# Eight heads at a time in an attention and feed-forward kernel, and identity products ahead of the first scores

## The chip, the cores and the metric

The kernel runs on one core of a Trainium2 chip. The metric is the device time of one execution in microseconds; the kernel before takes 1137.74 us (median of three runs, 1136.55 to 1138.45).

## The reference

A transformer block with adaptive LayerNorm. S = 2048 tokens, D = 1024, 32 query heads of width 32 that share one key and one value head, feed-forward width F = 3584, all in bf16. Cut to what matters:

```python
mod = (silu(c) @ w_mod).reshape(1, 6, 1, -1)      # sa, ca, ga, sb, cb, gb
h = layernorm(x) * (1 + ca) + sa
q = (h @ wq) -> 32 heads;  k = h @ wk;  v = h @ wv
p = softmax(q k^T / sqrt(32))
x = x + ga * ((p v) @ wo)
h = layernorm(x) * (1 + cb) + sb
return x + gb * ((silu(h @ w1) * (h @ w3)) @ w2)
```

## The kernel before

**Tiles.** The queries are cut into NB = 8 blocks of 256 tokens. `QT[:, n, f, :]` holds, for block n, four heads (f of 8) of 32 rows each, transposed: partition 32 g + d is row d of head g. `KT` holds the transposed keys four times over, once for each strip of 32 partitions. `V[:, k, :]` holds the values of key tile k (16 tiles of 128 keys). The normalised input, transposed, is `HT`; after the projections its memory is used again for feed-forward tiles.

**Attention.** The list `CYC` names 512 steps (n, f, j), each with four heads, 256 queries and 256 keys. For each step `s_exp` issues a burst of eight score products on TensorE: four heads in four row strips side by side, first for one key tile and then for the other, into four of the six PSUM banks of `S6`. Then come two exponentials on ScalarE (128x1024 each) into `U`, a ring of NU = 10 steps. Eight steps with one f are a unit (`av`): `pairs` adds the two key tiles of two steps on VectorE (128x2048), folds of 128x1024 bring these sums down, `dens` multiplies the last one by ones (row sums), `av_mm` multiplies `U` by `V` in four column strips, and `attend` transposes the row sums, takes their reciprocal, transposes back, copies the products from PSUM and writes their quotient over `QT[:, n, f]`. Units 0 and 1 run together in `two_units`.

**Rest of a block.** `wo` multiplies the eight `QT` tiles by the scaled output weights (32 products of 512 columns), adds to `X1`, and normalises; `slab` (14 a block) makes gate and up products, with a tanh on ScalarE for the silu; `quarter` (4 a block) multiplies by w2. The feed-forward of a block runs while the next block's attention does. Everything beside scores uses PSUM banks 6 and 7, until the last exponentials set the other six free.

**Order.** `Graph.op` collects operations with their dependences, an estimated time and a due time `vt`. `Placer` plays them through with these times and writes each engine's program in the order found, with semaphore waits. An operation may have several engines (`alts`); the one that starts first takes it. TensorE works in three array forms, "S" (scores, row strips), "A" or "C" (column strips) and "F" (whole array), and `SWITCH` prices a change between them. `PLAN` has 65 entries, one for each eight score steps: slacks for the choice and offsets on due times by tag and engine ("an/dve", "d10/sp"). Early projections carry estimates of their own (`cold`, 0.95, 1.7).

**The start.** Fourteen DMAs on the SyncE queue bring x, two fields of w_mod and wq in an order that the plan sets (tags d0 to d13). `lnt1` normalises a tile of 128 tokens and transposes it on TensorE; for tiles 0 to 5 the transposes go into the `S6` banks. `mod_cols` computes the scale and shift fields by products of one column, `scale0` scales the weights, `k_proj` and `q_proj` fill `KT` and `QT`. The first scores need tiles 0 and 1, both fields and the first two groups of wq.

Of the kernel before, what the change touches and what calls it, by code (L numbers as in the profile page):

```python
# [4 lines left out]
F32 = mybir.dt.float32  # L5
ACT = mybir.ActivationFunctionType
ALU = mybir.AluOpType
# [35 lines left out]
class Graph:  # L43
# [64 lines left out]
    def alias(self, new, old):  # L108
# [8 lines left out]
    (0, 0.08, 0.14, 0, 1.1, {"an/dve": 11, "av/dve": 9, "d0/sp": -38, "d1/sp": 10, "d10/sp": 222, "d11/sp": 2,  # L117
     "d12/sp": -4, "d13/sp": 2, "d2/sp": 51, "d3/sp": -151, "d6/sp": 67, "d7/sp": 32, "d8/sp": -29, "ev/act": -21,
     "k/pe": -26, "k/dve": 40, "ln/pe": -51, "ln/act": 32, "ln/dve": -11, "ln/pool": 57, "mc/pe": 57, "mc/sp": -2,
     "mod/pe": -62, "mod/dve": 10, "nm/act": 79, "pair/dve": -129, "q/pe": 3, "q/dve": -57, "quarter/pe": 11,  # L120
     "quarter/dve": -2, "s/pe": 67, "s/act": -3, "slab/pe": -5, "slab/act": 81, "slab/dve": 30, "v/pe": -8,
     "v/pool": 19, "wo/pe": -78, "wo/dve": 1, "wo/sp": 36}),
    (0, 0.11, 0.18, 2, 1.1, {"an/dve": 8, "av/pe": -111, "av/dve": 2, "d0/sp": -31, "d1/sp": 16, "d10/sp": -68,
     "d12/sp": 63, "d13/sp": -1, "d3/sp": -14, "d5/sp": 2, "d7/sp": -26, "d8/sp": -2, "ev/act": -29, "k/pe": -36,
     "k/dve": -9, "kb/pe": 72, "mod/dve": -5, "nm/act": 32, "pair/dve": -106, "q/pe": -4, "q/dve": -32,
     "quarter/dve": 2, "s/pe": 55, "s/act": 107, "slab/pe": -26, "slab/dve": 33, "slab/sp": 94, "v/pool": -34,
     "wo/pe": -77, "wo/dve": 4, "wo/pool": -59, "wo/sp": 22, "d11/sp": 0, "ln/pe": 0, "mod/pe": 0, "slab/act": 0}),
    (0, 0.25, 0.29, 0, 1.1, {"av/dve": 9, "d0/sp": -58, "d1/sp": 20, "d10/sp": 257, "d11/sp": -6, "d13/sp": 2,
     "d3/sp": -2, "d4/sp": 1, "d8/sp": 83, "ev/act": -11, "k/pe": -49, "k/dve": 1, "kb/dve": -7, "mc/pe": 63,
     "mc/sp": 5, "nm/act": 30, "out/sp": 1, "s/act": 114, "slab/sp": 4, "v/dve": 3, "v/pool": -26, "wo/pe": -78,  # L130
     "wo/dve": 14, "wo/pool": -23, "an/dve": 0, "d12/sp": 0, "d2/sp": 0, "mod/dve": 0, "pair/dve": 0,
     "quarter/pe": 0, "wo/sp": 0, "d5/sp": 0}),
    (0, 0.12, 0.29, 0, 3.5, {"an/dve": -3, "av/pe": -6, "av/dve": 6, "d12/sp": 20, "d4/sp": -21, "d9/sp": -6,
     "ev/act": -1, "k/pe": -62, "kb/dve": -3, "ln/pe": -2, "mc/pe": 77, "mod/dve": -9, "q/pe": -2, "q/dve": -56,
     "s/act": 2, "sc/dve": -14, "slab/act": 78, "slab/dve": 30, "slab/sp": 6, "wo/dve": 19, "d11/sp": 0,
     "mc/sp": 0, "s/pe": 0, "v/pool": 0, "wo/pe": 0, "wo/pool": 0, "out/sp": 0}),
    (0, 0.12, 0.21, 2, 2.5, {"an/dve": 49, "av/pe": -4, "d0/sp": -31, "d1/sp": 1, "d13/sp": -2, "d4/sp": -6,
     "d8/sp": 90, "ev/act": 38, "k/dve": -3, "mc/pe": 79, "nm/act": -1, "pair/dve": -93, "quarter/pe": 9,
     "slab/act": 70, "slab/dve": 33, "slab/sp": 18, "v/dve": -69, "v/pool": -4, "wo/pe": -6, "wo/dve": 1,
     "av/dve": 0, "d12/sp": 0, "k/pe": 0, "ln/dve": 0, "q/pe": 0, "d9/sp": 0, "sc/dve": 0}),  # L140
    (0, 0.12, 0.19, 1, 0.7, {"an/dve": -2, "av/pe": -8, "av/dve": 6, "d0/sp": -2, "d1/sp": 16, "d11/sp": 27,
     "d4/sp": -37, "d7/sp": -25, "k/pe": 1, "kb/pe": 5, "kb/dve": -4, "ln/pe": 4, "mc/pe": 143, "q/dve": -69,
     "quarter/pe": 12, "sc/dve": -12, "slab/pe": -27, "slab/dve": 32, "slab/sp": 13, "v/dve": 1, "wo/dve": 6,
     "wo/pool": 17, "d10/sp": 0, "mod/dve": 0, "nm/act": 0, "s/act": 0, "v/pool": 0}),
    (0, 0.12, 0.28, 0, 0.6, {"d10/sp": -68, "d3/sp": -46, "d8/sp": 83, "d9/sp": 72, "kb/pe": 2, "ln/dve": -11,
     "mc/pe": -7, "pair/dve": -16, "q/dve": -85, "q/sp": -6, "quarter/pe": 4, "slab/act": 82, "slab/dve": 33,
     "slab/sp": 16, "wo/pe": -5, "wo/dve": 3, "wo/pool": 15, "an/dve": 0, "d11/sp": 0, "v/pe": 0, "kb/dve": 0,
     "sc/dve": 0}),
    (0.16, 0.02, 0.28, 0, 2.1, {"av/dve": -2, "d10/sp": -85, "d11/sp": 1, "d4/sp": -32, "d5/sp": -18,
     "ev/act": -15, "kb/pe": -4, "ln/pe": -20, "ln/dve": -8, "ln/pool": 7, "mc/pe": 9, "mc/sp": 16, "mod/dve": -4,  # L150
     "nm/act": -31, "pair/dve": -79, "q/pe": -13, "quarter/pe": 2, "slab/pe": -22, "slab/dve": 31, "slab/sp": -62,
     "wo/pool": -40, "d0/sp": 0, "d7/sp": 0, "k/pe": 0, "slab/act": 0}),
    (0.14, 0.19, 0.09, 1, 2.1, {"d0/sp": -46, "d1/sp": 3, "d10/sp": -68, "d13/sp": 1, "d3/sp": -17, "d4/sp": -54,
     "d7/sp": -25, "d8/sp": 78, "k/pe": -1, "ln/dve": -11, "mc/pe": -28, "mc/dve": 25, "mod/pe": 4, "nm/act": -29,
     "pair/dve": -90, "q/pe": -2, "q/dve": -81, "quarter/pe": -10, "sc/dve": -1, "v/pe": -3, "v/dve": 5,
     "wo/pool": -18, "d11/sp": 0, "ev/act": 0, "mc/sp": 0, "mod/dve": 0, "d5/sp": 0, "kb/pe": 0}),
    (0.14, 0.17, 0.24, 1, 2.1, {"av/pe": -4, "d1/sp": 31, "d3/sp": 24, "d7/sp": -35, "ev/act": 20, "kb/pe": 6,
     "ln/dve": -16, "ln/pool": 60, "mc/pe": 2, "mc/dve": 35, "nm/act": -28, "pair/dve": -28, "q/dve": -49,
     "quarter/pe": -1, "slab/act": 10, "v/dve": 20, "wo/pool": -13, "av/dve": 0, "d0/sp": 0, "mod/pe": 0,
     "q/pe": 0, "slab/pe": 0}),  # L160
    (0.14, 0.16, 0.29, 1, 2.1, {"an/dve": -8, "d0/sp": -2, "d10/sp": -63, "d3/sp": 19, "d4/sp": -106, "kb/pe": 13,
     "ln/pe": 35, "ln/pool": 24, "mc/pe": -59, "mc/sp": -30, "mod/pe": 1, "nm/act": -45, "out/sp": -3,
     "pair/dve": 6, "q/pe": 4, "quarter/pe": 5, "sc/dve": 36, "v/pool": -11, "wo/sp": 1, "ln/act": 0, "mc/dve": 0}),
    (0.14, 0.16, 0.25, 1, 2.8, {"an/dve": -14, "d10/sp": -74, "d11/sp": -67, "d3/sp": -62, "d4/sp": -104,
     "d7/sp": -26, "ev/act": 41, "k/pe": 9, "kb/dve": 14, "ln/pe": 31, "ln/pool": -6, "nm/act": -24,
     "pair/dve": -10, "sc/dve": -24, "slab/pe": 4, "slab/dve": 21, "slab/sp": -61, "wo/pool": -17, "d0/sp": 0,
     "mc/sp": 0, "q/pe": 0, "slab/act": 0, "v/dve": 0}),
    (0.09, 0.26, 0.19, 1, 2.8, {"an/dve": -45, "d0/sp": -7, "d1/sp": 39, "d10/sp": -83, "d3/sp": 2, "d4/sp": -54,
     "d7/sp": -35, "k/pe": -94, "k/dve": -10, "kb/pe": 2, "ln/pe": -10, "ln/pool": -7, "mc/pe": -9, "mc/dve": 3,
     "nm/act": -23, "pair/dve": -3, "q/pe": -109, "quarter/pe": -3, "slab/dve": -32, "v/pool": -5, "wo/pe": -20,  # L170
     "d11/sp": 0, "slab/pe": 0, "av/pe": 0, "slab/sp": 0, "kb/dve": 0}),
    (0.09, 0.16, 0.25, 0, 2.8, {"d0/sp": -1, "d10/sp": -85, "d5/sp": -74, "k/dve": -7, "ln/pe": 4, "mc/pe": -11,
     "mc/sp": 2, "nm/act": -24, "pair/dve": -15, "slab/dve": -33, "v/dve": 1, "an/dve": 0, "d1/sp": 0, "ln/dve": 0,
     "quarter/pe": 0, "kb/pe": 0}),
    (0, 0.22, 0.2, 1, 2.4, {"d0/sp": 49, "d4/sp": -29, "k/pe": -87, "k/dve": -10, "mc/pe": -15, "nm/act": -13,
     "q/pe": -48, "slab/dve": -11, "slab/sp": -52, "v/dve": 2, "wo/pe": -83, "wo/dve": -12, "pair/dve": 0,
     "v/pool": 0, "d5/sp": 0}),
    (0, 0.13, 0.15, 1, 3.5, {"av/dve": -5, "d0/sp": 1, "d10/sp": -68, "d4/sp": -56, "d9/sp": 73, "k/pe": -82,
     "kb/pe": 4, "ln/pe": 16, "mc/pe": -12, "mc/sp": 14, "q/pe": -38, "slab/dve": 101, "slab/sp": 13, "wo/pe": -60,
     "d3/sp": 0, "ev/act": 0, "sc/dve": 0}),  # L180
    (0, 0.16, 0.15, 1, 3.1, {"av/dve": -7, "d10/sp": -70, "d11/sp": 19, "d4/sp": -25, "ev/act": 41, "k/pe": -32,
     "ln/pe": -17, "mc/pe": -16, "nm/act": -34, "pair/dve": -41, "slab/pe": -11, "slab/act": -11, "slab/sp": 4,
     "v/dve": -4, "wo/pe": -61, "slab/dve": 0, "kb/pe": 0, "wo/pool": 0}),
    (0.09, 0.14, 0.26, 1, 2.6, {"an/dve": -16, "av/dve": -5, "d11/sp": 14, "d12/sp": 26, "d3/sp": 64, "d4/sp": -22,
     "d5/sp": 13, "ev/act": 123, "k/pe": -87, "kb/pe": 25, "mod/dve": 2, "nm/act": -31, "pair/dve": -7,
# [400 lines left out]
def build(nc, x_in, wq_in, wk_in, wv_in, wo_in, w1_in, w3_in, w2_in, c_in, wmod_in, out, S, D, F):  # L586
# [110 lines left out]
    def pe_mm(n, cnt):  # L697
        return cnt * (n / 2400.0 + 0.0026) + 0.002
# [685 lines left out]
```

## Time and profile before

| | |
|---|---|
| median of three runs | 1137.74 us (1136.55 to 1138.45) |
| profiled execution | 1137.71 us, its span 1135.9 us |
| TensorE, VectorE, ScalarE busy | 1108.3, 992.1, 1021.3 us |
| TensorE clock granted | 0.998 of full, mean |
| DMA | 209.72 MB, mean 185 GB/s |
| first exponential starts | 33.74 us |
| last exponential ends | 1036.3 us |

In the views PE is TensorE, PEld its weight loads, DVE VectorE, ACT ScalarE, POOL GpSimd and SP SyncE. All operations are recorded by one helper, so every row shows L22, and groups are told apart by tiles: `S<-QT,KT` are scores, `U<-S` exponentials, `PB<-U,V` the P·V products, `PB<-PS,ONES` the row sums, `PS<-U` pairs and `PS<-PS` folds. The feed-forward products read `H20` in `HT` or `QT`, in which the normalised rows of the block before are kept. A row of the timeline has start, time, engine, operation, out<-in, array rows and columns, moving operand and count; a bracket tells how long the engine sat idle before it and who released it. Products overlap, so the time between two starts says more than the time of one.

### The profile page before, as it was taken

To read this page: it belongs to the slowest core of one execution; us is meant where nothing else is said; L and a number is where in the kernel's file an instruction comes from. 1 tells how busy PE (TensorE), PEld (TensorE's weight loads), DVE (VectorE), ACT (ScalarE), POOL (GpSimd) and SP (SyncE) were. 2 spreads that over 40 slices of the span, in tenths; PEclk is the share of its full clock that TensorE was granted. 3 is DMA by queue.
4 is the path that set the end of the run, shared out by engine and by line. 5 is a ranking of instruction groups with operands and counts; after the bars stand their busy time and mean duration, and the time that the engine had idled before them with its cause. 6 is when DMAs were issued, how large, how long until landed. Compare 5 with 4: busy or idle time off the path is not lost.

```text
span 1135.9 us, 38650 instructions
## 1 busy us (share of the span) xinstructions
PE 1108.3 (98%) x17512; PEld 757.2 (67%) x17512; DVE 992.1 (87%) x1614; ACT 1021.3 (90%) x1158; POOL 41.3 (4%) x92
## 2 busy tenths in 40 slices
PE   6899999999999999999999999999999999999998
PEld 6644446666567766777567766777577756776887
DVE  7988999998999889998998899988998889987532
ACT  5999999999999999999999999999999999994110
POOL 5200000000000000000000000000000000000000
PEclk9999999999999999999999999999999999999999
DMA  9320397665486658865596577768597568777993
GB/s 345 106 76 5 128 263 191 175 193 140 114 258 195 174 131 216 235 193 152 128 283 194 149 198 190 219 195 222 130 274 202 150 159 218 207 201 197 246 242 92
DMA packets 381540, 209.72 MB, mean 185 GB/s; under 512 B 17600, under 2 KB 373184, under 8 KB 381376
## 3 DMA queue, kind: packets, MB, share of 16 engines
q1 hardware_dynamic: 380944, 207.11, 65.8%
q8 instruction: 138, 2.26, 0.8%
q14 instruction: 26, 0.21, 0.1%
q10 hardware_dynamic: 432, 0.13, 0.0%
HBM read 199.89 MB, written 4.19 MB: 180 GB/s over the span
## 4 chain that ended last, share of the span: by engine, by line
PE 61%; ACT 25%; DVE 11%; issue 1%; POOL 1%; DMA 0%; DVEq 0%
PE PB L22 44%; ACT U L22 24%; PE S L22 16%; DVE PS L22 4%; DVE ST L22 2%; ACT HT L22 1%; DVE QT L22 1%; POOL RS L22 1%; DVE X L22 1%; DVE HT L22 1%; DVE RB L22 1%; DVE XNB L22 0%; DMA X<-in_A_x_dram 0%; DVE MV L22 0%; DVE RC L22 0%
## 5 line engine op out<-in xcount | busy, mean ns | idle before, releaser
L22 ACT ACTIVATE U<-S 128x1024 bf16<-128x1024 f32 x1024 | 964.6, 1131 | 7.2 <-PE S L22 6.3
L22 DVE TENSOR_TENSOR PS<-U 128x2048 bf16<-128x2048 bf16 x256 | 307.3, 1217 | 9.4 <-ACT U L22 7.9
L22 DVE TENSOR_TENSOR PS<-PS 128x1024 bf16<-128x1024 bf16 (+1 forms) x420 | 282.5, 690 | 3.4
L22 PE MATMUL PB<-QT,W 128*128 128x256 bf16 (+1 forms) x2992 | 229.8, 273 | 1.2 <-DVE HT L22 1.0
L22 PE MATMUL S<-QT,KT 32*128 32x256 bf16 x4096 | 203.8, 273 | 8.0 <-ACT U L22 5.0
L22 PEld LDWEIGHTS PB<-QT,W 128*128 128x128 bf16 (+1 forms) x2992 | 172.3, 97 | 44.3 <-issue 26.5
L22 PE MATMUL PB<-W2S,HT 128*128 128x256 bf16 x1512 | 188.4, 273 | 0.0
L22 PEld LDWEIGHTS PB<-W2S,HT 128*128 128x128 bf16 x1512 | 137.8, 98 | 39.4 <-issue 21.3
L22 PEld LDWEIGHTS S<-QT,KT 32*128 32x128 bf16 x4096 | 60.7, 92 | 139.8 <-ACT U L22 130.1
L22 PE MATMUL PB<-U,V 128*32 128x256 bf16 x4096 | 127.4, 273 | 0.9 <-ACT U L22 0.5
L22 PE MATMUL PB<-QT,HT 128*32 128x256 bf16 (+1 forms) x1560 | 116.0, 273 | 1.5 <-DVE HT L22 1.1
L22 PEld LDWEIGHTS PB<-U,V 128*32 128x32 bf16 x4096 | 101.6, 96 | 21.2 <-issue 12.7
L22 PE MATMUL PB<-HT,W 128*32 128x512 bf16 (+3 forms) x896 | 101.2, 336 | 0.1
L22 PEld LDWEIGHTS PB<-QT,HT 128*32 128x32 bf16 (+1 forms) x1560 | 85.3, 97 | 23.5 <-issue 14.1
L22 ACT ACTIVATE HT<-PB 128x512 bf16<-128x512 f32 (+1 forms) x105 | 74.4, 708 | 12.3 <-PE PB L22 12.3
L22 DVE SCALAR_TENSOR_TENSOR HT<-HT,PB 128x512 bf16<-128x512 bf16 x101 | 69.0, 684 | 8.1 <-ACT HT L22 8.0
L22 PEld LDWEIGHTS PB<-HT,W 128*32 128x32 bf16 (+1 forms) x896 | 51.1, 98 | 33.4 <-issue 10.5
L22 DVE TENSOR_TENSOR HT<-HT,PB 128x512 bf16<-128x512 bf16 x99 | 67.4, 681 | 2.5 <-PE PB L22 1.6
L22 ACT ACTIVATE HT<-S 128x512 bf16<-128x512 f32 (+1 forms) x16 | 11.5, 730 | 54.6 <-PE S L22 54.6
L22 DVE STREAM_TRANSPOSE RB<-PB 128x256 f32<-128x256 f32 x63 | 28.0, 444 | 37.3 <-PE PB L22 36.8
L22 PE MATMUL PB<-WO,QT 128*128 128x512 bf16 (+1 forms) x248 | 56.0, 381 | 1.1 <-DVE RB L22 1.1
L22 POOL TENSOR_SCALAR RS<-MV 128x1 f32<-128x1 f32 x32 | 11.6, 362 | 1004.5 <-DVE MV L22 1003.4
(107 smaller groups left out, 669.5 us busy)
## 6 DMA issues: line engine op xcount, KB each, us to landing
W<-in_B_w_dram SPq DMA_DIRECT2D x150, 512.0 KB, 4.6
W2S<-in_B_w_dram SPq DMA_DIRECT2D x30, 1792.0 KB, 8.5
HT<-in_B_w_dram SPq DMA_DIRECT2D x74, 512.0 KB, 4.6
W2S<-in_w_mod_dram SPq DMA_DIRECT2D x8, 1024.0 KB, 5.7
X<-in_A_x_dram SPq DMA_DIRECT2D x8, 512.0 KB, 7.5
U<-in_w_mod_dram SPq DMA_DIRECT2D x4, 1024.0 KB, 12.1
out_dram<-X SPq DMA_DIRECT2D x7, 512.0 KB, 7.4
W2S<-in_A_x_dram SPq DMA_DIRECT2D x5, 512.0 KB, 9.4
```

The source lines that it names most:

```text
L22: return getattr(e, call[0])(*call[1], **call[2])
```

## The change

In blocks 1 to 7 a unit has eight heads: `QT[:, n, f:f+2, :]`, that is 512 columns. `CYC` has (n, f, k) there, with f in steps of two and one key tile k of 128 keys a step, so a step has as many scores as before. `s_exp8` issues four products of 512 columns. `av8` replaces `av`: the unit's sixteen steps go in two halves of eight; `pair` adds two steps' key tiles (128x2048, in one piece), folds are 128x2048 and run over both halves; the first half's P·V products are copied from PSUM to `AVS` by ScalarE or VectorE, the second half's are added there; row sums, two transposes, reciprocal and multiply are done once for eight heads, twice as wide. Block 0 stays as it was.

`keep_warm` is new: for each whole-array operation of TensorE that the planner puts ahead of the first scores with an idle time of 0.2 us or more before it, it issues products of the identity by itself (128 columns, into bank 5), one for each 0.075 us of that idle time, once the identity is there. LayerNorm tile 5 leaves bank 5 and uses banks 6 and 7. The planner's estimates for early operations are the same as for later ones, the fixed part of a product's estimate goes from 0.0026 to 0.0042 us, and all 65 entries of `PLAN` are new, so the order differs throughout.

```diff
-    (0, 0.08, 0.14, 0, 1.1, {"an/dve": 11, "av/dve": 9, "d0/sp": -38, ...
+    (0, 0.15, 0.06, 1, 2.5, {"an/act": -4, "an/dve": 9, "av/dve": 1, ...
...
+        if e == "pe" and self.warm and self.step == 0 and n.mode == "F":
+            self.keep_warm(start)
...
+    def keep_warm(self, start):
+        product, need = self.warm
+        gap = start - max(self.t["pe"], need.fin)
+        if not need.done or gap < 0.2:
+            return
...
+        sem, count = self.sem, int((gap - 0.05) / 0.075)
...
+            for _ in range(count):
+                play(eng, product(REC))
...
-        return cnt * (n / 2400.0 + 0.0026) + 0.002
+        return cnt * (n / 2400.0 + 0.0042) + 0.002
...
-        static = tt < 6
+        static = tt < 5
...
-    CYC += [(n, f, j) for n in range(NB) for f in range(NC) for j in range(NJ) if n or f > 1]
+    CYC += [(0, f, j) for f in range(2, NC) for j in range(NJ)]
+    CYC += [(n, f, k) for n in range(1, NB) for f in range(0, NC, 2) for k in range(NTT)]
...
+    def s_exp8(c, n, f, k, r, bk):
+        def mm():
+            return [lambda e, g=g: e.matmul(
+                BANK[2 * r[g // 2] + g % 2], KT[32 * g:32 * (g + 1), k * P:(k + 1) * P],
+                QT[32 * g:32 * (g + 1), n, f:f + 2, :].rearrange("p f q -> p (f q)"), start=True, stop=True,
+                tile_position=(32 * g, 0)) for g in range(4)]
+        op("pe", mm, 0.207, reads=[("KT", k // 2), ("QT", n, f), ("QT", n, f + 1)], writes=bk, vt=TOP + c, mode="S", post=0.171)
+        exp2(c, r)
...
+    def av8(n, f):
...
+        for half in range(2):
+            for k in range(8 * half, 8 * half + 8):
+                s_exp(c0 + k)
+            for q in range(8 * half, 8 * half + 8, 2):
...
+                op("dve", lambda m=m, k0=k0: [lambda e: e.tensor_tensor(
+                    PS[:, k0:k0 + 2].rearrange("p k h q -> p (k h q)"), U[:, m].rearrange("p h k q -> p (h k q)"),
+                    U[:, m + 1].rearrange("p h k q -> p (h k q)"), ALU.add)], 1.12,
...
+                if q:
+                    fold(c, p, p + 2)
...
+                        BANK[b][32 * h:32 * (h + 1), :], V[:, k, :], U[:, (c0 + k) % NU, h].rearrange("p k q -> p (k q)"),
...
+            if half == 0:
+                op("act", lambda b: [lambda e: e.activation(AVS, BANK[b], ACT.Copy)], 0.5, reads=[("av", u, 0)],
+                   writes=avs, vt=c0 + 8.0, sess=s,
+                   alts=[("dve", lambda b: [lambda e: e.tensor_copy(AVS, BANK[b])], 0.605)])
+            else:
+                op("dve", lambda b: [lambda e: e.tensor_tensor(AVS, AVS, BANK[b], ALU.add)], 0.605, reads=[("av", u, 1)] + avs,
+                   writes=avs, vt=c0 + 8.0, sess=s)
...
+    pl.warm = (lambda e: e.matmul(BANK[5][:, 0:P], IDENT[:], IDENT[:], start=True, stop=True), ident)
```

More of the change, by code (lines that the diff above doesn't have):

```diff
@@ new lines @@
+    (0, 0.12, 0.16, 1, 0.6, {"an/dve": -16, "d0/sp": -53, "d10/sp": 222, "d4/sp": -5, "ev/act": 2, "mod/dve": -11,
+     "nm/act": -31, "out/sp": -4, "pair/dve": -76, "q/dve": -85, "quarter/pe": -6, "s/act": -25, "v/dve": 8,
+     "wo/pe": -3, "wo/sp": -15, "sc/dve": 0, "d12/sp": 0, "kb/pe": 0}),
+    (0, 0.17, 0.16, 0, 3, {"d10/sp": 284, "d12/sp": -5, "d2/sp": -97, "d3/sp": 16, "d4/sp": 64, "d8/sp": 23,
+     "d9/sp": -3, "k/dve": 4, "kb/pe": -7, "nm/act": -37, "pair/dve": -40, "q/pe": -49, "q/dve": 5,
+     "quarter/dve": 2, "s/pe": -11, "s/act": -6, "slab/act": 14, "wo/pool": -25, "wo/sp": -17, "ev/act": 0,
+     "mod/dve": 0, "wo/pe": 0}),
@@ new lines @@
+    (0.02, 0.12, 0.23, 0, 1.7, {"an/act": 41, "av/pe": -32, "d0/sp": -59, "d10/sp": 177, "d13/sp": 66, "d3/sp": 1,
+     "d5/sp": 53, "d9/sp": -19, "ev/act": 4, "k/pe": 5, "ln/pool": -13, "mc/pe": 108, "mod/dve": -13,
+     "pair/dve": -12, "q/pe": 1, "quarter/pe": 37, "quarter/dve": -68, "quarter/sp": 14, "slab/act": -54,
+     "wo/pe": 7, "d7/sp": 0, "wo/dve": 0, "s/pe": 0}),
+    (0.02, 0.15, 0.23, 3, 2.2, {"an/act": 1, "av/dve": 73, "d12/sp": -7, "d3/sp": -15, "d5/sp": 51, "d7/sp": 65,
+     "k/dve": 5, "kb/pe": -47, "out/sp": -1, "q/dve": -4, "quarter/pe": 29, "quarter/sp": 13, "s/pe": 7,
+     "v/pool": -1, "wo/dve": 3, "mod/dve": 0}),
@@ new lines @@
+    (0.06, 0.12, 0.27, 1, 2.4, {"av/pe": -9, "av/dve": 20, "d13/sp": 67, "d3/sp": -4, "d4/sp": -2, "d5/sp": 47,
+     "d6/sp": -21, "d7/sp": 65, "d9/sp": 2, "ev/act": 16, "ln/pool": -25, "mc/dve": 69, "mod/pe": -6,
+     "quarter/dve": 7, "wo/sp": 102}),
+    (0.06, 0.11, 0.25, 1, 2.4, {"av/pe": -8, "av/dve": 12, "kb/dve": -29, "ln/dve": 2, "out/sp": -3, "slab/pe": 1,
+     "v/pool": -3, "wo/sp": 81, "quarter/dve": 0}),
+    (0, 0.13, 0.29, 1, 0.4, {"d0/sp": -58, "d13/sp": 65, "d6/sp": -30, "ln/pool": -13, "pair/dve": -11,
+     "v/pool": 1, "d10/sp": 0, "s/act": 0, "kb/dve": 0}),
@@ L308 @@
+    (0.06, 0.11, 0.2, 0, 3.2, {"an/act": -48, "d1/sp": -1, "ev/act": -3, "ln/pe": 49, "ln/dve": 94, "mc/pe": 101,
+     "mc/dve": 69, "mc/sp": 11, "pair/dve": -18, "q/pe": -80, "quarter/pe": 81}),
 ]
@@ L802, in tr @@
                 IDENT[:]) for cc in range(NC)]
-        op("pe", tr, 0.95 if tt < 4 else 0.6, reads=[("XN", slot), "IDENT"], writes=bk, vt=vt, mode="F", sess=s, post=0.145)
+        op("pe", tr, 0.6, reads=[("XN", slot), "IDENT"], writes=bk, vt=vt, mode="F", sess=s, post=0.145)
         dst = HT[:, :, tt * P:(tt + 1) * P]
```

470 lines of the change are left out of this document (256 added, 214 removed).

## The prediction

> **What bounds the kernel now.** I read the page first, then the engines' busy time over one middle block, then the timelines of ScalarE and TensorE inside a block and after the last exponential, and the first 40 us last.
>
> ```profile
> span 1135.9 us, 38650 instructions
> PE 1108.3 (98%) x17512; PEld 757.2 (67%) x17512; DVE 992.1 (87%) x1614; ACT 1021.3 (90%) x1158; POOL 41.3 (4%) x92
> ```
> ```profile
> 640.00:766.00 126.00, 125.28 (x2044) 85.37 (x2036) 116.03 (x184) 124.43 (x143) 3.55 (x4) 1.00 0.69 189
> ```
> The profiled execution took 1137.71 us, 1.8 us more than its span and 0.03 us less than the median of the runs (1137.74), so I sum against 1137.7. The second row is one block of 256 queries, from one output projection to the next, 126 us. Its columns are PE, PEld, DVE, ACT and POOL. Three engines are nearly full, so who sets the pace must be worked out from starts, since a busy time contains overlap.
>
> ```profile
> 596.69 6.59 ACT L22 ACTIVATE U<-S 128x1024 bf16<-128x1024 f32 x7
> 603.02 0.75 ACT L22 ACTIVATE HT<-PB 128x512 bf16<-128x512 f32 x1
> 603.49 3.03 ACT L22 ACTIVATE U<-S 128x1024 bf16<-128x1024 f32 x3
> ...
> 1029.68 6.57 ACT L22 ACTIVATE U<-S 128x1024 bf16<-128x1024 f32 x7
> ```
> Seven exponentials start-to-start take 603.02 - 596.69 = 6.33 us, 0.904 each, and a tanh 0.47. A block has 128 exponentials and 14 tanh: 122.3 us. ScalarE therefore leaves 3.7 us of each 126.
>
> ```profile
> 58.64 1.48 PE L22 MATMUL PB<-HT,W 128*32 128x512 bf16 x24
> 60.05 0.40 PE L22 MATMUL S<-QT,KT 32*128 32x256 bf16 x8
> ...
> 165.92 1.47 PE L22 MATMUL PB<-WO,QT 128*128 128x512 bf16 x6
> 167.32 0.40 PE L22 MATMUL S<-QT,KT 32*128 32x256 bf16 x8
> ...
> 1022.83 1.93 PE L22 MATMUL PB<-U,V 128*32 128x256 bf16 x64
> 1024.69 0.40 PE L22 MATMUL S<-QT,KT 32*128 32x256 bf16 x8
> ...
> 1026.77 1.48 PE L22 MATMUL PB<-W2S,HT 128*128 128x256 bf16 x12
> 1028.18 0.40 PE L22 MATMUL S<-QT,KT 32*128 32x256 bf16 x8
> 1028.51 0.29 PE L22 MATMUL PB<-PS,ONES 128*32 128x256 bf16 x4
> 1028.74 1.27 PE L22 MATMUL PB<-W2S,HT 128*128 128x256 bf16 x10
> ```
> Read starts, not durations. A burst of scores (8 products) holds TensorE for 0.33 us (1028.18 to 1028.51); the P·V products of one unit of four heads, 64 of them, 1.86; the row sums, 4 products, 0.23; 12 full-width products and the change back to scores 1.41; six 512-wide ones 1.40. Let x be a full-width product of 256 and s the change of array form: 12x + s = 1.41. The six 512-wide ones give 6y + s = 1.40. With s about 0.10, x is 0.109 and y 0.216. A block then needs 64 x 0.33 (scores) + 8 x 1.86 (P·V) + 8 x 0.23 (sums) + 672 x 0.109 (feed-forward) + 32 x 0.216 (output projection) + 56 x 0.10 (changes back, for the bursts that a P·V row does not follow) = 21.1 + 14.9 + 1.8 + 73.2 + 6.9 + 5.6 = 123.5 us, 98% of 126. So TensorE sets the block's pace by a little, ScalarE is 1.2 us behind it, and VectorE (116.03 busy) has about a tenth free. That closeness is the core of this case: what TensorE saves, ScalarE can cash only until its own 122.3 us.
>
> ```profile
> 1057.87 3.66 PE L22 MATMUL S<-QT,HT 128*128 128x256 bf16 x32
> ```
> The exponentials end at 1029.68 + 6.57 = 1036.3; from there 99.6 us remain. They are a chain (sums, output projection, LayerNorm; the block's first feed-forward product stands at 1057.87), 672 x 0.109 = 73.2 us of feed-forward, and the last writes. This tail hardly shrinks when TensorE gets cheaper. The end therefore moves only as the last exponential moves.
>
> **The change, part by part.** *Units of eight heads.* In blocks 1 to 7, 448 score bursts become 4 products of 512 columns instead of 8 of 256. Columns are equal; what goes is one of two rounds of starting. From the rows, four column-strip products side by side cost, at 512 columns, (1.41 - 0.10)/6 = 0.218 for 24/4 rounds, against two 256 rounds of (1.86 - 0.10)/8 = 0.220: 2 ns less. The upper bound: the sums' single round costs 0.23 and half a score burst without its change of form is (0.33 - 0.10)/2 = 0.115, against 0.109 for a steady round, so 6 ns of start-up per round, 12 per burst, may go. Lower bound 0 (same columns, same form), nearest row 2 ns, upper 12. I take 8, since the score burst has just two rounds and the first of them is the dear one: 64 x 8 ns = 0.5 us a block. P·V: eight pairs of rounds per half, 64 x 2 ns = 0.15. Row sums: eight visits of 0.23 become four of 0.23 + 0.107, for 256 more columns: 1.84 to 1.35, 0.5 less. Sum 1.15 us a block, 8.0 over seven.
>
> The Trainium skill, page "TensorE: Matmul & The Clock Gate", section "Wait — 56ns, not 53.3ns?", gives a fixed cost of about 2.5 ns for each product beside its columns. By that the score bursts would save 64 x 2.5 = 0.16 us a block instead of 0.5, and the sum over seven blocks would be 5.6 and not 8.0; the full-width rows agree with it (2 x 0.109 against 0.216), the score bursts I put above it.
>
> *VectorE.*
> ```profile
> L22 DVE TENSOR_TENSOR PS<-PS 128x1024 bf16<-128x1024 bf16 x416 | 277.6, 685 | 3.4
> L22 DVE STREAM_TRANSPOSE RB<-RC 128x256 f32<-128x256 f32 x64 | 28.5, 445 | 2.1
> L22 DVE TENSOR_TENSOR QT<-RB 128x256 bf16<-128x256 f32 x64 | 27.1, 424 | 1.9
> L22 DVE COPY RB<-PB 128x256 f32<-128x256 f32 x62 | 26.1, 421 | 4.9 <-PE PB L22 4.3
> L22 DVE TENSOR_TENSOR PS<-PS 128x2048 bf16<-128x2048 bf16 x4 | 4.9, 1216 | 0.0
> ```
> Two old units: 14 folds x 0.685 + 2 x (2 x 0.445 + 0.424 + 0.421) = 9.6 + 3.5 = 13.1 us, the small reciprocals left aside in both. One new unit: 7 x 1.216 = 8.5; two transposes, a multiply and an add at twice the width, each between one and two old prices, 1.7 to 3.5 in all; the copy of the first half 0.4 to 0.8 unless ScalarE takes it. That is 10.2 to 12.8 us, so 0.3 to 2.9 less per eight heads, 1 to 12 a block. VectorE is not the bound, so I cost it at nothing; it loosens the waits behind it.
>
> *ScalarE.* The copy of the first half (128x512 from PSUM) may run on either engine. On ScalarE I price it as the tanh of the same shape, 0.47: 28 copies are 0 to 13.2 us on an engine that will have 126 - 1.15 - 122.3 = 2.5 us a block. I take a third of them, nine (VectorE is the emptier engine), 4.2 us, half of it in the slack: +2.1. Behind a copy on ScalarE the next exponential queues, and with it TensorE's next burst.
>
> *The end.* The new chain from row sums to `QT` has two wider transposes and a wider multiply ahead of the last output projection: at most 0.9 + 0.4 us, less the three small folds that become one; +0.7.
>
> *The first 40 us.*
> ```profile
> U<-in_w_mod_dram SPq DMA_DIRECT2D x1, 1024.0 KB, 14.5
> ...
> 5.69 2.47 SPq L22 DMA_DIRECT2D U<-in_w_mod_dram  x1
> ...
> 21.55 2.06 PE L22 MATMUL PB<-SCC,U 128*128 128x1 bf16 x32
> ...
> 34.82 1.35 PE L22 MATMUL PB<-SAB,W 128*128 128x1 bf16 x48 [0.21 <-DVE KT L22]
> ...
> 31.45 0.47 DVE L22 TENSOR_SCALAR QT<-PB,QBI 128x256 bf16<-128x256 f32 x1
> ...
> 33.74 1.01 ACT L22 ACTIVATE U<-S 128x1024 bf16<-128x1024 f32 x1
> ```
> The same kind of product still runs at half speed at 21 us: 32 one-column products take 2.06 us at 21.55, 48 take 1.35 at 34.82. Such small work, then, does not wake it. The change fills its predicted gaps with 128-wide identity products. If these wake it, the second half of the shift field (issued 5.69, landed 5.69 + 14.5 = 20.2) is multiplied from 20.3 instead of 21.55 and in 0.9 instead of 2.06: 2.4 us earlier; the K and Q projections behind add about 1.5. Against that, the evacuation into `QT` (31.45) takes its turn on VectorE among the LayerNorm statistics, which are not shortened. So the first exponential, 33.74 now, comes 0 to 6 us earlier; below nothing, identity products cold and still in TensorE's in-order queue may cost 1 us. I take 3.5. Block 0 is paced by exponentials (ScalarE is busy throughout, the fourth pair of the row below), so this shift reaches the end whole.
> ```profile
> 100.00:150.00 50.00, 49.82 (x956) 24.73 (x958) 46.16 (x80) 50.00 (x56) 0.00 (x0) 1.00 0.30 101
> ```
> What becomes late next is VectorE's statistics.
>
> The Trainium skill, page "TensorE: Matmul & The Clock Gate", section "Part 4: PE-mode transpose", says that transposes do not count as busy for the clock; the rows here agree so far that transposes and one-column products alone had not brought full speed by 21.55.
>
> *The new order.* The list of offsets decides which product stands before which burst. No row prices it. Bounds: the order now loses 126 - 123.5 = 2.5 us a block on TensorE; a better one can gain at most that (17 us over seven), a worse one lose as much. I take 0.
>
> Sum: -3.5 - 8.0 + 2.1 + 0.7 = -8.7, so **1129.0 us**.
>
> **Rivals.**
> 1. *All of it is cashed and the waits shrink too.* VectorE's relief and 1.15 us of room cut the 2.5 us of lost TensorE time by a third, 0.9 a block: -6, and copies stay on VectorE, -2.1: 1121. For: VectorE at 116 of 126. Against: ScalarE's 122.3 is near.
> 2. *ScalarE holds the pace.* TensorE's saving becomes waiting for score banks:
> ```profile
> PEld S L22 <- ACT U L22: 130.1, 468, 1.7
> ```
> Weight loads already wait 0.28 us on average before a burst. Then only the start counts: 1134.2.
> 3. *The identity products do nothing* (still half speed) and the rest is eaten as in 2: within 0.2% of 1137.7.
> 4. *Slower: ScalarE gets the copies.* If the order gives it most of the 28, ScalarE needs 122.3 + 1.9 = 124.2 a block, and as it never ran a block closer than 3.7 us, the block is 127.9: seven blocks +13, less 3.5 at the start: 1147. It decides above about 15 copies (15 x 0.47 = 7 us). For: ScalarE is the first named engine for it and the tail cannot absorb a late last exponential. Against: VectorE has more room. A half of this is 1142.
>
> **How the numbers follow.** Forecast (1124 to 1132) 0.40; rival 1 0.16; rival 2 0.16; rival 3 0.07; rival 4 0.21. A measurement of this kernel can tell about 0.2%, 2.3 us, from no change. Faster: 0.40 + 0.16 + 0.16 = 0.72; within 0.07; slower 0.21. Leaving half of rival 4 and the far side of rival 1 outside, the range is 1118 to 1142; the forecast's own is 1124 to 1132.
>
> **What would show it.** Right: first exponential near 30 us; 32 one-column products in about 0.9 us before 20 us; score bursts x4 with under 0.33 us to the next start; row sums 28 visits fewer; block period near 125; few `HT` copies of 128x512 f32 on ACT; tail still near 100 us. Wrong: a period of 126 or more with ScalarE at 124 and more, a first exponential after 33 us, or a longer tail.

## The result, and the profile after

The changed kernel takes 1150.19 us (median of four, 1149.13 to 1151.18) against 1138.1 for the kernel before in the same series: a ratio of 1.0109, 95% interval 1.0091 to 1.0126. It is 12 us slower, where 9 us faster was forecast, and it lies above the range, which ended at 1142. The profiled execution took 1151.18 us, 1.8 more than its span; it is the longest of the four, so what is summed below comes to 13.5 us and not to 12. First the page: span, engines, and the row of the granted TensorE clock.

```profile
span 1149.4 us, 29666 instructions
PE 1121.8 (98%) x13120; PEld 708.3 (62%) x13144; DVE 978.8 (85%) x1298; ACT 1024.3 (89%) x1167; POOL 43.6 (4%) x91
PEclk8999988999999999999999999999999999999999
```
Four thousand products fewer, VectorE 13 us less busy, ScalarE 3 us more, TensorE still at 98%. The busy times alone show no loss. Next are the same stretches as in the prediction (columns PE, PEld, DVE, ACT, POOL, clock), with 10 us of the start added.

```profile
640.00:766.00 126.00, 124.49 (x1460) 76.21 (x1460) 114.19 (x141) 124.12 (x143) 2.49 (x4) 1.00 0.68 186
100.00:150.00 50.00, 48.66 (x847) 22.37 (x840) 43.02 (x64) 50.00 (x56) 0.00 (x0) 1.00 0.01 2
20.00:30.00 10.00, 9.87 (x122) 9.21 (x121) 7.16 (x19) 3.97 (x4) 4.70 (x6) 0.50 1.07 372
```
In the same 126 us of the middle, TensorE and ScalarE are as full as before, and no engine has been freed. The third row is new: 20 to 30 us from the start the clock stands at half although TensorE is busy for 9.87 of 10 us. (For before the same row reads 1.00, but eight transposes take 1.05 us there at 23.47, as at half clock: until the first change of clock that the profile recorded, this column says nothing, and the time of like instructions decides.)

Where the time went is read from the starts of the exponentials, counted along ScalarE's `U<-S` rows. The first and the last rows of after are these.

```profile
35.30 1.02 ACT L22 ACTIVATE U<-S 128x1024 bf16<-128x1024 f32 x1
...
1042.62 4.76 ACT L22 ACTIVATE U<-S 128x1024 bf16<-128x1024 f32 x5
```
| | before | after | after - before |
|---|---|---|---|
| first exponential starts | 33.74 | 35.30 | +1.6 |
| from there to the 129th (block 0) | 121.1 | 122.7 | +1.7 |
| to the 1024th (blocks 1 to 7) | 880.3 | 888.2 | +7.9 |
| to the end of the span | 100.8 | 103.2 | +2.4 |

Each part loses something, block 0 too, whose units the change did not touch. Inside blocks 1 to 7 the loss is not even. From the first exponential of a block to the first of the next (for block 7, to its last) they take, in us:

| block | 1 | 2 | 3 | 4 | 5 | 6 | 7 |
|---|---|---|---|---|---|---|---|
| before | 125.5 | 125.4 | 126.0 | 126.5 | 126.4 | 125.2 | 125.4 |
| after | 127.6 | 125.0 | 126.2 | 126.6 | 127.3 | 127.5 | 127.9 |

Units of eight heads stand in all seven. Blocks 2 to 4 take the same time with them as with four heads, within 0.4 us each; blocks 1, 6 and 7 lose 2.2 to 2.6 us each. A cost of the units themselves should show in every block. Within blocks 1 to 7 I summed TensorE's time from each start to the next, by kind of product (us):

| | window | scores | P·V | row sums | all else |
|---|---|---|---|---|---|
| before | 880.3 | 150.7 | 108.3 | 10.6 | 610.2 |
| after | 888.2 | 156.7 | 107.5 | 9.9 | 613.6 |

From the start of a burst to the next start of something else the scores take 6 us more, although they were to save most. It is not the products: where TensorE does not idle behind a burst, the next work starts 330 ns after a narrow burst and 327 ns after a wide one (medians; bursts with feed-forward or projection products behind them). What grew is waiting, behind some bursts and inside a few. All else takes 3.4 us more; 4.1 of that are products of the modulation (`PB<-SCC,W2S`), of which after leaves 128 for block 1 (5.0 us) and before 32 (0.9 us). The order put them there; the rest of the 256 run in block 0, where ScalarE hardly waits for TensorE (it idles 0.7 us in all). Idle time of TensorE between products is 10.9 us in this window before and 17.7 after, in many small pieces. The waits (total us, times, longest us) show two of the sources.

```profile
PEld S L22 <- ACT U L22: 149.0, 476, 1.7
...
DVE PS L22 <- ACT U L22: 24.4, 51, 1.2
...
PE S L22 <- ACT U L22: 7.3, 17, 1.4
```
TensorE waits 7.3 us for ScalarE to free score banks, 5.0 before. VectorE's pairs wait 24.4 us for exponentials, 7.9 before. Little of this reaches TensorE: the row sums idle 1.9 us in all for VectorE, 0.2 before, at two places:

```profile
830.03 0.40 PE L22 MATMUL PB<-PS,ONES 128*32 128x512 bf16 x4 [0.65 <-DVE HT L22]
...
956.24 0.40 PE L22 MATMUL PB<-PS,ONES 128*32 128x512 bf16 x4 [1.15 <-DVE PS L22]
```
The brackets are TensorE's idle time before the row sums. Only the second waits for the sums themselves, the first for another tile of VectorE. In both the product that stands next in TensorE's program was put there by the planner for a time at which VectorE was not yet done.

### The profile page after: what moved, and what is told of

Read it like the earlier page. It is cut to its first block, busy times and chain, and to the rows that moved or that the text cites. A ratio compares the mean times of both kernels' runs of the same rounds, so it can differ in the third digit from the quotient of the medians.

```text
span 1149.4 us, 29666 instructions
## 1 busy us (share of the span) xinstructions
PE 1121.8 (98%) x13120; PEld 708.3 (62%) x13144; DVE 978.8 (85%) x1298; ACT 1024.3 (89%) x1167; POOL 43.6 (4%) x91
## 4 chain that ended last, share of the span: by engine, by line
ACT 42%; PE 39%; DVE 14%; issue 2%; POOL 1%; DMA 1%; SPq 0%; DVEq 0%
ACT U L22 40%; PE PB L22 28%; PE S L22 12%; DVE PS L22 7%; ACT HT L22 2%; DVE HT L22 2%; DVE QT L22 1%; DVE ST L22 1%; POOL RS L22 1%; DMA U<-in_w_mod_dram 1%; DVE X L22 1%; DVE RB L22 1%; DVE XNB L22 0%; DVE WO L22 0%; SPq L22 0%
## 5 line engine op out<-in xcount | busy, mean ns | idle before, releaser
L22 DVE TENSOR_TENSOR PS<-U 128x2048 bf16<-128x2048 bf16 x256 | 311.6, 1219 | 26.6 <-ACT U L22 24.4
L22 DVE TENSOR_TENSOR PS<-PS 128x2048 bf16<-128x2048 bf16 (+1 forms) x224 | 260.0, 1162 | 3.4
L22 PE MATMUL S<-QT,KT 32*128 32x512 bf16 (+1 forms) x2304 | 203.5, 362 | 10.8 <-ACT U L22 7.3
L22 PEld LDWEIGHTS S<-QT,KT 32*128 32x128 bf16 x2304 | 52.7, 91 | 157.3 <-ACT U L22 149.0
L22 PE MATMUL PB<-U,V 128*32 128x512 bf16 (+1 forms) x2272 | 128.0, 359 | 2.5 <-DVE HT L22 1.2
L22 PE MATMUL PB<-QT,HT 128*128 128x256 bf16 (+1 forms) x1408 | 122.9, 273 | 1.4 <-DVE HT L22 1.3
L22 DVE TENSOR_TENSOR HT<-HT,PB 128x512 bf16<-128x512 bf16 (+1 forms) x129 | 88.1, 683 | 25.2 <-PE PB L22 23.5
L22 ACT ACTIVATE HT<-PB 128x512 bf16<-128x512 f32 (+2 forms) x114 | 77.7, 682 | 34.8 <-PE PB L22 34.5
L22 PEld LDWEIGHTS PB<-QT,HT 128*128 128x128 bf16 (+1 forms) x1408 | 90.8, 97 | 27.6 <-issue 16.3
L22 PEld LDWEIGHTS PB<-U,V 128*32 128x32 bf16 x2272 | 52.5, 96 | 58.2 <-issue 16.1
L22 PEld LDWEIGHTS PB<-WO,QT 128*128 128x128 bf16 (+1 forms) x256 | 20.2, 99 | 26.5 <-issue 8.0
```

The lines of the kernel that those rows point to most:

```text
L22: return getattr(e, call[0])(*call[1], **call[2])
```

## The experiments

### Without the identity products

```diff
-        if e == "pe" and self.warm and self.step == 0 and n.mode == "F":
-            self.keep_warm(start)
```


> The changed kernel without the identity products; every other instruction and its order stay as they are. Theory A (the clock: the products woke TensorE at 7.5 us but it fell back at 17.7 and stayed at half speed until 31.4, so they bring nothing to the first exponential): first exponential within 0.7 us of 35.3 and total 1149 to 1152. Theory B (the products stand in the queue ahead of real work and are themselves the delay of the first exponential, 33.7 to 35.3): first exponential back at 34 or earlier, total 1146 to 1149.

Measured: 1149.83 us, ratio 1.0109 [1.0091, 1.0126], as with them. TensorE's timeline (start, time, operation, idle):

```profile
13.95 1.08 PE L22 MATMUL S<-IDENT,XNB 128*128 128x128 bf16 x8 [2.87 <-ACT XNB L22]
14.83 2.06 PE L22 MATMUL PB<-SCC,U 128*128 128x1 bf16 x32
```
The first exponential starts at 33.15, 2.15 us ahead of after's, as theory B had it, and the profiled execution keeps this lead: its last exponential is 2.0 us ahead. The medians differ by 0.4 us only, as theory A had it. The two agree because after's own start varies: two kernels below with the same early program start at 33.7. So the identity products do not make the 12 us, and bring nothing either. What they do to the clock is seen beside the same rows of after:

```profile
14.66 0.67 PE L22 MATMUL S<-IDENT,XNB 128*128 128x128 bf16 x8
15.80 2.10 PE L22 MATMUL PB<-SCC,U 128*128 128x1 bf16 x32 [0.48 <-DMA U<-in_w_mod_dram]
17.77 1.05 PE L22 MATMUL S<-IDENT,XNB 128*128 128x128 bf16 x8
```
Eight transposes take 0.67 us at 14.66, so the clock was woken, and 1.05 at 17.77, so it was lost again. The 32 products with the field take 2.10 in between, at the full clock, and 2.06 in the kernel without identity products, where transposes take 1.08. They don't follow the clock.

### The clock held through the start, and through block 1

```diff
+        if e == "pe" and self.warm and self.step == 0 and n.tag == "ln":
+            product = self.warm[0]
...
+                for _ in range(8):
+                    play(eng, product(REC))
...
-                BANK[b][:, k:k + 1], WM0[:, c, fld * D:(fld + 1) * D]..., SCC[:, 3, c:c + 1], ...
+                BANK[b][:, 64 * k:64 * k + 64], WM0[:, c, fld * D:(fld + 1) * D]...,
+                SCC[:, 3, c:c + 1].broadcast_to([P, 64]), ...
```


> The changed kernel with more real work on TensorE ahead of the first scores, in the same order: each one-column product of the two early fields streams 64 equal columns, and eight identity products follow each LayerNorm transpose. If half speed between 17.7 and 31.4 us is what made the start late (theory A): clock 1.00 from 7.5 us on, first exponential 31 to 33 and total down by 2 to 4 us, 1146 to 1148. If the start is late because the order was made with a price of 1.0 us for 32 field products that take 2 (theory B): clock held, but first exponential still 34 to 35.5 and total 1149 to 1151.

Measured: 1151.74 us, 1.0121 [1.0105, 1.0138]. The clock and two groups of field products, now 64 columns wide:

```profile
20.00:30.00 10.00, 9.42 (x151) 9.08 (x150) 6.65 (x20) 3.88 (x5) 4.63 (x6) 1.00 1.07 372
```
```profile
15.58 2.11 PE L22 MATMUL PB<-SCC,U 128*128 128x64 bf16 x32
19.77 2.07 PE L22 MATMUL PB<-SCC,U 128*128 128x64 bf16 x32
```
At full clock, and with 64 columns for one, 32 field products take what they took, and the first exponential starts at 33.96, which is not ahead of 33.15 without identity products. The start isn't bound by the clock. The total lies above both theories; block 0 takes 125.0 us here, 122.7 in after.

In another kernel the one-column products of the modulation, half of which run in block 1, were made 64 columns wide, with twelve identity products behind each group, to keep the clock up from 164 to 192 us:

```diff
-            BANK[b][:, k:k + 1], WMB[r][:, cc, k * P:(k + 1) * P], SCC[:, 3, cc:cc + 1], ...
+            BANK[b][:, 64 * k:64 * k + 64], WMB[r][:, cc, k * P:(k + 1) * P],
+            SCC[:, 3, cc:cc + 1].broadcast_to([P, 64]), ...
+            lambda e: e.matmul(BANK[b][:, 256:384], IDENT[:], IDENT[:], start=True, stop=True)] * 12, ...
```


> The changed kernel with more real work in the eight chunks of the modulation (64 equal columns for each one-column product and twelve identity products behind each chunk), in the same order. Theory A (half speed at 164.5 to 171.3 and 185.0 to 191.8 us costs time that is never won back): no stretch of half speed after 35 us, the 256th exponential 1 to 3 us earlier than 285.7, total 1147 to 1149. Theory C (TensorE waits there for exponentials and for the modulation chunks anyway, by the order): clock held, the 256th exponential within 0.7 us, total 1149.5 to 1151.5.

Measured: 1152.7 us, 1.0134 [1.0113, 1.0155]. Clock and time by window:

```profile
150.00:200.00 50.00, 42.53 (x666) 22.99 (x658) 43.54 (x80) 46.07 (x52) 3.64 (x4) 1.00 0.78 227
```
After has 0.86 here. The half speed is gone and nothing is won: the total is above both theories, blocks 1 to 7 take 888.3 us (888.2 in after), block 0 125.3 (122.7). What the clock alone is worth there this edit can't tell, since it adds products, and a run of them breaks off for 1.7 us at 167.46.

### The copies of the first half

In after, 8 of the 28 copies ran on ScalarE. Two kernels play the changed kernel's order from a list, with the copies all on VectorE, then all on ScalarE.

```diff
+ORDER = """4 0 10 1 3 5 8 2 6 7 ... 102 74 33.1 103 71 ..."""
```


> The changed kernel with its order written out, and the eight copies of a first half that ScalarE does (of 28) moved to VectorE at the same place in the order. Theory F (copies on ScalarE set its pace, rival 4 of the prediction): 8 x 0.48 = 3.8 us or more faster, 1144 to 1147. Theory C: within 1.5 us of the changed kernel, since eight copies are hidden in ScalarE's slack, 1149 to 1151.

> The changed kernel with its order written out, and all 28 copies of a first half on ScalarE, at the same place in the order. 20 more copies of 0.48 us are 9.6 us. If ScalarE has slack for them (3.7 us a block, theory C): 0 to 3 us slower, 1150 to 1153. If ScalarE is the pace (theory F): 7 to 11 us slower, 1157 to 1161.

Measured: 1150.27 us, 1.0103 [1.0088, 1.0118], with none on ScalarE; 1158.65, 1.0175 [1.016, 1.019], with all. ScalarE's groups (busy, mean ns, idle before), of the second:

```profile
L22 ACT ACTIVATE HT<-PB 128x512 f32<-128x512 f32 x28 | 19.8, 707 | 1.9 <-PE PB L22 1.9
```
Twenty copies more cost 1158.65 - 1150.19 = 8.5 us, 0.42 each, about what the prediction priced; within their own series the two kernels lie 8.4 apart. So rival 4 is a real mechanism, but not this kernel's: the eight that it has cost nothing. With none on ScalarE the last exponential of the profiled execution starts within 0.1 us of after's.

### The wide products cut back, in the same order

```diff
-            return [lambda e, g=g: e.matmul(
-                BANK[2 * r[g // 2] + g % 2], ..., QT[32 * g:32 * (g + 1), n, f:f + 2, :].rearrange("p f q -> p (f q)"),
-                ...) for g in range(4)]
+            return [lambda e, g=g, x=x: e.matmul(
+                BANK[2 * r[g // 2] + g % 2][:, x * B:(x + 1) * B], ..., QT[32 * g:32 * (g + 1), n, f + x, :],
+                ...) for x in range(2) for g in range(4)]
...
-                        BANK[b][32 * h:32 * (h + 1), :], V[:, k, :], U[:, (c0 + k) % NU, h].rearrange("p k q -> p (k q)"),
+                        BANK[b][32 * h:32 * (h + 1), x * B:(x + 1) * B], V[:, k, :], U[:, (c0 + k) % NU, h, x, :],
```


> The changed kernel with every 512-column score product and P.V product of blocks 1 to 7 cut into two of 256 columns, in the same order. If the wider products save time as I reckoned (8 ns a score burst, 2 ns a step of P.V): 448 x 10 ns = 4.5 us slower, 1154 to 1155. If they save only the 3 ns of one start each (theory D: mis-sized): 2 to 3 us slower, 1152 to 1153. If the wide products themselves hurt (theory E): faster than 1149.

Measured: 1154.65 us, 1.0157 [1.0128, 1.0185], 4.5 more than after. By the sum this is what the prediction gave the wide scores and P·V, 7 x 0.65 = 4.6. The profile says otherwise. TensorE's timeline of this kernel:

```profile
240.38 0.60 PE L22 MATMUL PB<-HT 128*32 128x256 bf16 x13
242.34 0.73 PE L22 MATMUL PB<-HT 128*32 128x256 bf16 x19 [1.36 <-issue]
...
585.93 1.26 PE L22 MATMUL PB<-QT,W 128*32 128x256 bf16 x37
588.48 0.95 PE L22 MATMUL PB<-QT,W 128*32 128x256 bf16 x27 [1.30 <-issue]
...
714.43 1.04 PE L22 MATMUL PB<-QT,W 128*32 128x256 bf16 x29
716.93 1.16 PE L22 MATMUL PB<-QT,W 128*32 128x256 bf16 x35 [1.46 <-issue]
```
Three times a run of like products breaks off for 1.3 to 1.5 us with nothing released: 4.1 us. Set beside after's, the exponentials fall back by 4.6 us at these places and by 0.7 in all the rest of blocks 1 to 7. Each such run consists of column-strip products, 27 ns from start to start, behind P·V products just as short. So I cut scores and P·V apart.

> The changed kernel in its own order, only the score products of blocks 1 to 7 cut back from 512 to 2 x 256 columns (448 bursts, 1792 products more); P·V stays 512 wide. e4_split, which cuts both, lost 4.5 us, and three rows of its timeline explain 4.1 of it by stalls: 240.38, 585.93 and 714.43 each show a run of column-strip fill products (27 ns each, right behind P·V products that are as short) broken by 1.36, 1.30 and 1.46 us with nothing released ('issue'). Theory P (each wide score burst saves 8 ns, as the prediction has it): 448 x 8 = 3.6 us more than the changed kernel, 1153.8, spread over the blocks evenly, 0.5 each. Theory Q (a burst saves only the 3 ns between 327 and 330 of the starts, and e4's loss is the three stalls, which come of short products in dense runs): 0 to 1.5 us more, 1150.2 to 1151.7, and no stall over 1 us put down to issue inside column-strip runs.

> The changed kernel in its own order, only the P·V products of blocks 1 to 7 cut back to 2 x 256 columns (1792 products more); scores stay 512 wide. Theory P (P·V saves 2 ns a round, 0.15 us a block): 1.1 us more, 1151.3, no stall. Theory Q (dense short products stall the issue): the three stalls of e4_split stay in the same places, 1.3 to 1.5 us each, so 3 to 5 us more, 1153 to 1155.

Measured: scores alone 1151.51 us, 1.0119 [1.0102, 1.0136], 1.3 more; P·V alone 1154.66, 1.0145 [1.013, 1.0161], 4.5 more. The 1.3 us are 3 ns for each of 448 bursts, within what the intervals leave open of zero. 8 ns would have given a ratio of 1.0141, just outside this kernel's interval, but after's ratio has an interval of its own; the traces decide. In the profiled executions of after and of this kernel the first exponential starts at 35.30 and 35.29, the last at 1046.2 and 1046.4: 0.2 us for 448 bursts, where 8 ns each would make 3.6. So theory P falls for the scores. For P·V the loss is theory Q's, but its places are not: the profiled execution, the shortest of its four (1153.39), has one such stall, elsewhere. Below are three rows of it, then the engines' row (PE, PEld, DVE, ACT, POOL, clock) of the time right behind, and then the same place in after.

```profile
996.69 1.93 PE L22 MATMUL PB<-U,V 128*32 128x256 bf16 x64
998.45 1.04 PE L22 MATMUL PB<-QT,W 128*32 128x256 bf16 x31
1001.41 0.27 PE L22 MATMUL PB<-QT,W 128*32 128x256 bf16 x1 [1.92 <-issue]
```
```profile
1003.00:1006.00 3.00, 3.00 (x19) 1.67 (x18) 0.14 (x2) 1.96 (x3) 0.00 (x0) 0.58 0.60 176
```
```profile
998.19 1.91 PE L22 MATMUL PB<-U,V 128*32 128x512 bf16 x32
999.93 1.05 PE L22 MATMUL PB<-QT,W 128*32 128x256 bf16 x32
```
With 32 wide P·V products ahead the same run passes without a break; with 64 short ones it stalls before its last product. Behind the stall the clock is low for some us (0.58 in the row above), and the exponentials fall back by 3.6 us at this place, against 0.3 in all the rest of blocks 1 to 7. What wide P·V products save here is thus mostly such stalls. Their number seems to differ between executions, which these profiles, one each, cannot show. What makes them stays open: in before all P·V products are short, and none of its column-strip runs breaks off; of the kernels with four heads below, e11 has one such stall (1.41 us at 835.04).

### Order against unit size

The planner adds up its own estimates while it writes the order. With the estimates that each kernel ships, it ends at 1126.8 us for before and 1134.2 for after: the changed kernel is 7.4 us worse by its own reckoning, order and units together. At like estimates it has blocks 1 to 7 of after 5.4 us longer, and much where the chip has it: 1.1, 1.0 and 2.2 us in blocks 1, 6 and 7, 0.5 in blocks 2 to 4 together. To separate the order from the unit size I gave both nearly the same estimates (0.0026 us a product, 0.216 for a wide burst, 1.92 for 32 field products, slow early products), and searched `PLAN` anew from a neutral start, with the same method and time; no identity products. The kernel with eight heads is called e5, that with four e6.

```diff
-PLAN = [ ... ]
+PLAN = [ ... 65 other entries ... ]
```


> Units of eight heads as in the changed kernel, without the identity products, with prices corrected from the profiles (32 field products 1.92 us, score bursts 0.216, 0.0026 beside a product's columns, slower early operations) and a PLAN searched anew from 65 equal entries, with as many trials as for the next kernel. Theory C (the loss lies in the order that PLAN makes, not in the units): within 4 us of e6_four_equal, rather below it; both 1143 to 1152. Theory E (units of eight heads are themselves slower, by waits that an order can't mend): 8 to 15 us above e6_four_equal.

> The kernel before, with units of four heads, the field products' price corrected to 1.92 us, and a PLAN searched from 65 equal entries with as many trials as for e5_eight_equal. Theory C: a less finished order costs it about what the changed kernel lost, 1143 to 1152, and it stands at or up to 4 us above e5_eight_equal. Theory E: 8 to 15 us below e5_eight_equal.

Then with a longer search of another kind (entry by entry, many plans kept side by side). The one for eight heads set out from plans that such a search had found from neutral, the one for four from a plan searched out of the kernel before's; the two had the same length. They are e10 and e11.

> Eight-head units without identity products, as in e5_eight_equal, but the plan is searched much longer, so that the kernel's own planner, at the same prices for both unit sizes, ends at 1130.3 instead of 1137.2 (e5) and 1135.6 (the changed kernel's order at these prices). Theory C (the order found by the search is what the change lost): measured time less planner's figure was 15.5 us for e5 and 14.6 for the changed kernel, so 1130.3 + 14.6 to 15.5 gives 1145 to 1146, 4 to 5 us under the changed kernel, with the last exponential 5 us or more earlier. Theory E (eight-head units cost time themselves and the order hardly counts): within 2 us of 1150. Theory G (a longer search only fits the planner's prices and not the chip): 1149 to 1153.

> Four-head units, as in e6_four_equal, plan searched as long as in e10_eight_long; the planner ends at 1128.4 instead of 1138.0 (e6). Theory C: measured less planner's was 13.4 us for e6 and 10.5 for the kernel before (whose order ends at 1127.5 at these prices), so 1139 to 1142. Theory E: as the kernel before, 1136 to 1139, whatever the order (but e6 with 1151.4 speaks against that). Theory G: near e6, 1149 to 1153. If e10 and e11 differ by no more than the 1.9 us by which the planner tells them apart plus 2, unit size is worth little either way; if e10 stays 4 us or more above what the planner tells, eight-head units carry a price that the planner does not have.

| kernel | units | planner, like estimates | measured, ratio and interval | first exp. | blocks 1 to 7 |
|---|---|---|---|---|---|
| before | four | 1127.5 | 1138.1, 1 | 33.74 | 880.3 |
| e11 | four | 1128.4 | 1142.62, 1.0043 [1.0028, 1.0058] | 33.14 | 881.0 |
| e6 | four | 1138.0 | 1151.36, 1.0111 [1.0096, 1.0127] | 34.16 | 892.2 |
| e10 | eight | 1130.3 | 1148.37, 1.0091 [1.0075, 1.0108] | 31.66 | 883.7 |
| after | eight | 1135.6 | 1150.19, 1.0109 [1.0091, 1.0126] | 35.30 | 888.2 |
| e5 | eight | 1137.2 | 1152.74, 1.0122 [1.0105, 1.0139] | 33.42 | 893.3 |

Kernels of four heads that differ in nothing but the order (and, with it, the engine of an operation that may run on several) lie 12.9 us apart in one series: before with 1138.47 and e6 with 1151.36. That is as much as the change's whole loss. With four heads the measured time follows the planner's. With eight it does so in rank only: the planner has e10 5.3 us under after, and the chip 1.8.

With the first, shorter search the sizes are 1.4 us apart, with the longer one 5.75; with the orders that the kernels ship they are 12. So theory E's 8 to 15 us between e5 and e6 fall, and theory G falls: the longer search brought 8.7 us with four heads and 4.4 with eight. Theory C holds in part. Its 1145 to 1146 for e10 was missed: 1148.4 is inside the 2 us around 1150 that theory E gave. Its 1139 to 1142 for e11 was missed by 0.6. An order can thus cost all that the change lost, and blocks 2 to 4 show units of eight heads that cost nothing; but the best order found for eight heads won back only 1.8 us, and how the 12 us divide between order and units stays open.

Measured less planner's is 10.6 to 14.2 us with four heads and 14.6 to 18.1 with eight. This looks like 3 to 4 us that the planner does not price in units of eight heads, but two things keep it from being shown. Kernels of four heads alone scatter by 3.6 us. And the estimates were not quite the same: kernels with four heads keep longer ones for the first two query projections (twice and 1.5 times the plain estimate). Put into e10's order, the early estimates of e11 move its end from 1130.3 to 1131.8, so that the planner tells the two 3.4 us apart and not 1.9, of 5.75 measured. In the profiled executions the rest sits in three places: the planner has e10's first exponential 3.6 us ahead of e11's (2.1 with like early estimates), and the chip gives 1.5; blocks 1 to 7 take 2.7 us more and not 0.9; the end 2.6 and not 1.3. What makes the last two was not settled, and neither was whether a better order would bring eight heads under 1138: none of these did. The waits rule out one candidate. Rows of e10 and of e11:

```profile
PEld S L22 <- ACT U L22: 144.8, 475, 0.8
```
```profile
PEld S L22 <- ACT U L22: 129.4, 469, 1.6
```
This looks like rival 2, but the row stands near 129 in all kernels with four heads and between 144 and 149 in those with eight (159 with all copies on ScalarE), and at 135.5 in the kernel with P·V cut back, where it is 13.5 us lower than in after and nothing is won. So it doesn't tell where the time goes; scores hold TensorE 153.9 us in e10's blocks and 152.7 in e11's.

## Why the prediction was wrong

**The new order: the step that failed.** The prediction wrote "No row prices it", gave bounds of 17 us to each side, took 0, and then let neither bound into the range. Measured, two orders of one and the same kernel lie 12.9 us apart, more than any other term of the sum, and the loss of the changed kernel stands in blocks 1, 6 and 7 and not in 2 to 4, which have the same units. The term had a price that could have been had: the planner's own end, 7.4 us later for the changed kernel, and 8.1 at like estimates (1127.5 and 1135.6), with the units in it. How much of the 12 us is order alone was not separated.

**The blocks, -8.0: mis-sized.** Scores were given 8 ns a burst, 3.6 us; cutting them back costs 1.3 by the medians and 0.2 by the traces. The reason given, a dear first round, does not hold: what stands behind a burst starts 0.32 to 0.33 us after it in both kernels.

```profile
643.23 0.40 PE L22 MATMUL S<-QT,KT 32*128 32x512 bf16 x4
643.55 1.49 PE L22 MATMUL PB<-QT,W 128*128 128x256 bf16 x12
```
The Trainium skill, page "TensorE: Matmul & The Clock Gate", section "Wait — 56ns, not 53.3ns?", has about 2.5 ns of fixed cost for each product; by it the prediction's estimate was 64 x 2.5 ns a block, 1.1 us in seven. The medians agree: 330 and 327 ns, 3 ns for the round that goes. The row sums were to save 3.5 us: a visit held 0.18 us before (10.6 us, 59 visits in the window) and not 0.23, and holds 0.32 now (9.9 us, 31), so 0.7 is saved. P·V saves 0.8 (1.1 forecast, though 64 x 2 ns is 0.13 a block and 0.9 in seven) beside the stalls. In all less than 3 us of 8.0, and the waits took more than that.

**The start, -3.5: wrong.** It rested on the field products running at half speed, from 32 that took 2.06 us and 48 others that took 1.35. Those are different products: the field's take 2.1 us at either clock. The identity products did wake the clock and did not keep it. The +1.6 of the table isn't firm: the kernel with P·V cut back has the same start, and its first exponential stands at 33.67. What held is that a shift of the start reaches the end whole: without identity products the lead is 2.15 us at the first exponential and 2.0 at the last.

**ScalarE's copies, +2.1; the end, +0.7.** Eight copies came where nine were assumed, at a cost of nothing rather than 2.1; half of their price was put on the path, and none of it was. The end is 2.4 us longer, and between e10 and e11 2.6; but from the last exponential on e6 takes 97.5 us and e11 103.1, both with four heads, so the order moves it as well. It was not tried alone.

**The rivals.** Rival 3 came true in part: the identity products brought nothing, though they did wake the clock for 10 us. Rival 4 came true in its sign alone. No rival said that the list of offsets itself is worse.

## What to carry to other kernels

Where an order is searched, a change that replaces both a structure and its searched order is two changes, and the second can be the larger: price the order by the planner's own end, keep its bounds in the range, and compare structures only after equal searches. When undoing a part costs just what was reckoned, read the timeline before believing the reckoning: nearly all of the 4.5 us here were stalls and not the price of products. And compare the speed of an engine at two times only by the same instruction on the same operands.

## What the runs showed that was not expected

- Products of one column with the field's weights take 2.1 us for 32, about 60 ns each from start to start, at full clock (15.80) as at half, and with 64 columns too; 48 with the query weights took 1.35 us, 28 ns each. The field's weights are read with a stride, which may be the reason; it was not tried.
- The clock, once woken by 77 identity products (transposes 0.67 us), fell back to half at about 17.7 us while TensorE was busy without a break with transposes, field products and three identity products at a time. The Trainium skill, page "TensorE: Matmul & The Clock Gate", section "Part 4: PE-mode transpose", says that transposes do not count as busy for the clock; the 0.50 from 20 to 30 us agrees. With eight more identity products behind each transposed tile, and field products 64 columns wide, the clock held. But e11, which has no identity products, was awake for a while as well: eight transposes take 1.06 us at 14.50 and 0.68 at 17.28, after nothing but transposes and field products. Which work counts is therefore open, and so is the prediction's "such small work, then, does not wake it".
- Long runs of products at 27 ns from start to start can break off for 1.3 to 1.9 us with nothing released; the profile shows no cause.

The rows of e11 that the second point rests on:

```profile
14.50 1.06 PE L22 MATMUL S<-IDENT,XNB 128*128 128x128 bf16 x8
15.35 2.07 PE L22 MATMUL PB<-SCC,U 128*128 128x1 bf16 x32
17.28 0.68 PE L22 MATMUL S<-IDENT,XNB 128*128 128x128 bf16 x8
```
